# One decode step of attention and a gated feed-forward layer: batch rows packed side by side, K turned in one piece, fewer VectorE and GpSimd instructions

## The chip, the cores and the metric

The kernel runs on one core of a Trainium2 chip. The metric is the device time of one execution in microseconds (us); lower is better. Engines: TensorE (PE in the profile, PEld for its weight loads), VectorE (DVE), ScalarE (ACT), GpSimd (POOL), SyncE (SP), which here only issues loads, and sixteen DMA engines that move data between HBM and the on-chip memory (SBUF). Matrix products land in eight banks of PSUM.

## The reference

Four sequences (B = 4) each decode one token of width D = 576. Attention has 32 query heads, 16 key/value heads of width 128, and looks at the last 4096 of 16384 cached positions:

```python
W = min(4096, max(256, Sk // 4))                 # 4096
q = (layernorm(x) @ wq).reshape(B, 1, 32, 128).transpose(0, 2, 1, 3)
k = jnp.repeat(k_cache[:, :, Sk - W:, :], 2, axis=1)
v = jnp.repeat(v_cache[:, :, Sk - W:, :], 2, axis=1)
p = softmax(einsum("bhqd,bhkd->bhqk", q, k) * 128 ** -0.5)
h = x + einsum("bhqk,bhkd->bhqd", p, v).reshape(B, 1, 4096) @ wo
n = layernorm(h)
gate = n @ W_gate                                # 576 x 4608
out = h + ((gate * (gate > 0)) * (n @ W_up)) @ W_down
```

All inputs are bf16. The window of K is 4 x 16 x 4096 x 128 elements, 67 MB, and V as much; the weights are another 25 MB. Each byte is used once or by a few rows only.

## The kernel before

**Loads.** All large loads are issued by SP in one fixed order (`place`, `add_kv`, lines 219 to 290): wq, then K tiles 0 to 4, then V and K tiles in turn, the last four V tiles, wo, W_gate, W_up and W_down. One K or V tile is 4.19 MB: four heads of one sequence over the whole window (16 tiles each). K and V go round a ring of four slots in `arena`. Before SP issues a load it waits for the last reader of the place: the score products of a K tile (`QK`) or the value products of a V tile (`PV`). The weights at the end use slots that the last tiles release.

**Order of work.** Each engine runs its instructions in program order; the lists are written by `Prog`, with semaphore waits derived from named dependencies. The main loop goes over the 16 K tiles g, with batch b = g // 4:

- `turn_k` (line 427): VectorE turns the K tile in place by 32x32 blocks, taken as 32-bit words. A tile takes two instructions of 4096 columns (`TRA`). In tiles 4, 8 and 12 other work lies between the two.
- `pe_qk` (434): TensorE makes the scores of the tile, 32 products, once the second turn is done. Four tiles fill banks 0 and 1 with a batch's scores (128 x 1024).
- `soft` (459 to 480), once per batch: VectorE takes the row maximum (`MAX`), the maximum per head by two small turns (`MT`, `GM`, `GM1`, `MB`), scales it (`NB`); ScalarE takes exp in two halves of 512 with row sums (`EXP`); VectorE turns the two halves (`PTR`).
- `remap` (483 to 501): TensorE moves the probabilities to the layout that the value products need (`RM`), into banks 6 and 0; ScalarE copies the first half (`EV` 0, line 500), VectorE the second (`EV` 1, line 497), each in four copies, one per mask column of `m4`, into `pT`.
- `pe_pv` (504): 32 value products per V tile into banks 2 to 5. V runs four tiles behind K.
- `select_o` (524 to 536): the wanted rows of these banks, times the softmax weights `fm`, summed into `o_sel`, by ScalarE (line 529) and VectorE (532, 535, 536). It is put off until after the next K turn (`late`, `flush`).
- `weights` (540 to 551), once per batch: adds the two row sums (`WL`), spreads them over a mask (`FQ`), a product with `toq` on TensorE (`F4M`), reciprocal (`F4`), and `fm` (`FM`).

**Around it.** GpSimd makes masks and constants at the start (lines 293 to 336), among them `toq` by 16 selects (line 329); VectorE finishes some of them. After the loop come the output projection with wo, the second layer norm, gate and up products (line 675), the gated product `HH` (684), its transposes (690), the down projection (713), two final copies (716, 717) and two output stores of four rows each (720). In the feed-forward part the four batch rows stand in columns 0, 8, 16 and 24 of `hnT`, `sel4` and `xsel`, so the four output rows lie eight partitions apart.

Of the kernel before, what the change touches and what calls it, by code (L numbers as in the profile page):

```python
# [11 lines left out]
B = 4  # L12
# [110 lines left out]
def bass_sequential_preLN__sliding_block_cached__glu_gated_reglu__decode_kernel(  # L123
# [12 lines left out]
    with ExitStack() as es:  # L136
# [47 lines left out]
        gmh = sb("gmh", [128, 8], FP32)  # L184
        fq = sb("fq", [128, 4], FP32)
        f4 = sb("f4", [128, 4], FP32)
# [7 lines left out]
        xsel = sb("xsel", [B, 32], BF16)  # L194
# [97 lines left out]

        pool("c_idb0", lambda e: e.memset(ident_b[:, :], 0.0))
# [33 lines left out]
        pool("c_toq0", lambda e: e.memset(toq[:, :, :, :], 0.0))  # L327
        for q in range(16):
            pool(f"c_toq{q + 1}", lambda e, q=q: e.affine_select(out=toq[:, :, :, :], in_=toq[:, :, :, :],  # L329
                                                               pattern=[[0, 16], [-32, 4], [-1, 2]], compare_op=ALU.not_equal,  # L330
                                                               fill=1.0, base=-2 * q, channel_multiplier=1), [f"c_toq{q}"])
        pool("c_xs0", lambda e: e.memset(xsel[:, :], 0.0))
        pool("c_xs1", lambda e: e.affine_select(out=xsel[:, :], in_=xsel[:, :], pattern=[[-1, 32]], compare_op=ALU.not_equal,
                                                fill=1.0, base=0, channel_multiplier=8), ["c_xs0"])
        pool("c_oT", lambda e: e.memset(oT[:, :, :], 0.0))
        pool("c_hnT", lambda e: e.memset(hnT[:, :, :], 0.0))
        dve("c_eps", lambda e: e.memset(eps_c[:, :], EPS))
# [60 lines left out]
        def dve_x():  # L398
            dve(None, lambda e: e.tensor_copy(out=xnT[:, 0:4, 0:4], in_=tpv[:, 0:16].rearrange("p (c b) -> p c b", b=B)),
                ["TP1", "c_xnT"])  # L400
            for a in range(2):
                dve("xnT", lambda e, a=a: e.tensor_scalar(out=xnT[:, 4 + a, 0:4], in0=tpv[:, 16:20], scalar1=par[:, a:a + 1],
                                                          scalar2=None, op0=ALU.mult), ["c_par"])
            dve("xT", lambda e: e.tensor_copy(out=xT[:, :, :], in_=tpv[:, 32:52].rearrange("p (c b) -> p c b", b=B)))
# [22 lines left out]
        def turn_k(g, w):  # L427
            k = arena[:, land[("K", g)] + w * QWW:][:, 0:QWW].bitcast(FP32)
            dst = k.rearrange("p (n h l a) -> p n l h a", h=2, l=2, a=2)
            src = k.rearrange("p (n l h a) -> p n l h a", h=2, l=2, a=2)  # L430
            dve(("TRA", g, w), lambda e: e.transpose(out=dst, in_=src), [("L", "K", g)] if w == 0 else [])  # L431


        def pe_qk(g):
            b, qd = divmod(g, 4)
            for cb in range(4):
                for w in range(2):
                    for a in range(4):
                        deps = []
                        if cb == w == a == 0:  # L440
                            deps = [("TRA", g, 1)]
                            if g == 0:
                                deps.append("QW")
                            if qd == 0 and b:
                                deps += [("EXP", b - 1, 1), ("MAX", b - 1), ("EV", b - 1, 1)]
# [13 lines left out]
        def row_max(b):  # L459
            dve(("MAX", b), lambda e: e.tensor_reduce(out=hx[:, 0:1], in_=psb[:, 0:2, :].rearrange("p a b -> p (a b)"),  # L460
                                                      axis=AX.X, op=ALU.max, negate=True), [("QK", 4 * b + 3), "c_hx", ("NB", b - 1) if b else None])

        def head_max(b):
# [4 lines left out]
            dve(("GM1", b), lambda e: e.tensor_copy(out=hy[:, :].rearrange("p (d i q) -> p d i q", i=4, q=2),  # L468
                                                    in_=bass.AP(tensor=gmh, offset=0, ap=[[8, 128], [2, 4], [0, 4], [1, 2]])), [("GM", b)])
            dve(("MB", b), lambda e: e.transpose(out=hx[:, :], in_=hy[:, :]), [("GM1", b)])  # L470
            dve(("NB", b), lambda e: e.tensor_scalar(out=stat[:, b, 1:2], in0=hx[:, 0:1], scalar1=SCALE, scalar2=None, op0=ALU.mult),  # L471
                [("MB", b)])

        def exps(b):
            for w in range(2):
                act(("EXP", b, w), lambda e, w=w: e.activation(  # L476
                    out=p_sb[:, 512 * w:512 * w + 512], in_=bank[w], func=ACT.Exp, bias=stat[:, b, 1:2], scale=SCALE,
                    accum_out=stat[:, b, 5 + w:6 + w]), [("NB", b), ("PTR", b - 1, 1) if b else "QT"] if w == 0 else [])
            for w in range(2):
                dve(("PTR", b, w), lambda e, w=w: e.transpose(out=p2[:, 512 * w:512 * w + 512], in_=p_sb[:, 512 * w:512 * w + 512]),  # L480
                    [("EXP", b, w), ("RM", b - 1, 1) if b else None])

        def remap(b):
            for n in range(4):
                for i in range(4):
# [4 lines left out]
                        ([("PTR", b, 1), "c_tov", ("EV", b - 1, 0) if b else None] if n == 0 else [("EXP", b, 0)]) if n % 2 == i == 0 else [])  # L490
            for h in range(2):
                for a in range(4):
                    out_ = bass.AP(tensor=pp, offset=16 * h + 2 * a, ap=[[PPW, 128], [8, 2], [32, 128], [1, 2]])
                    src = bank[0 if h else 6].rearrange("p (n c q) -> p n c q", n=2, q=2)
                    deps = [("RM", b, h), ("PV", 4 * b - 1) if b else "QMM"] if a == 0 else []
                    if h:
                        dve(("EV", b, 1), lambda e, out_=out_, src=src, a=a: e.tensor_scalar(  # L497
                            out=out_, in0=src, scalar1=m4[:, a:a + 1], scalar2=None, op0=ALU.mult), deps)
                    else:
                        act(("EV", b, 0), lambda e, out_=out_, src=src, a=a: e.activation(  # L500
                            out=out_, in_=src, func=ACT.Copy, scale=m4[:, a:a + 1]), deps + (["c_m4"] if a == 0 else []))
# [38 lines left out]
        def weights(b):  # L540
            dve(("WL", b), lambda e: e.tensor_tensor(out=stat[:, b, 13:14], in0=stat[:, b, 5:6], in1=stat[:, b, 6:7], op=ALU.add),
                [("EXP", b, 0), ("EXP", b, 1)])
            dve(("FQ", b), lambda e: e.tensor_scalar(out=fq[:, :], in0=qm[:, :], scalar1=stat[:, b, 13:14], scalar2=None,  # L543
                                                     op0=ALU.mult), [("WL", b), "c_qm"])
            pe(("F4M", b), lambda e: e.matmul(m_ps[:, 0:4], lhsT=toq[:, :, :, :].rearrange("p j t h -> p (j t h)"), rhs=fq[:, :],  # L545
                                              start=True, stop=True), [("FQ", b), "c_toq16", "QT", "qkeep0", "qkeep1"])
# [24 lines left out]
        dve("c_sel", lambda e: e.tensor_reduce(out=sel4[:, 0:32:8], in_=c_s4[:, :, :], axis=AX.X, op=ALU.max),  # L571
            ["c_s41", "c_sel0"])
        for q in range(4):
            dve("c_selc", lambda e, q=q: e.tensor_copy(out=selc[:, q, :, q], in_=e8[:, :]), ["c_e8", "c_selc0"])
# [19 lines left out]
        for g in range(NTILE):  # L594
            turn_k(g, 0)
            if g == 4:
                soft(0)
            if g and g % 4 == 0:
                remap(g // 4 - 1)
            turn_k(g, 1)  # L600
# [12 lines left out]
        act("warm_sqrt2", lambda e: e.activation(out=warm[:, 0:1], in_=eps_c[:, :], func=ACT.Sqrt), [("EXP", B - 1, 1)])  # L613
# [139 lines left out]
```

## Time and profile before

| what | value |
|---|---|
| four runs | 380.13, 381.44, 380.27, 379.94 us; median 380.2 |
| profiled execution | 380.13 us, of which the span of the profile is 378.3 us |
| bytes read | 159.6 MB, 422 GB/s over the span |
| VectorE busy | 231.2 us, of which 140.7 us in the 32 K turns (4.43 us each) |
| TensorE busy | 210.9 us at a mean granted clock of 0.80 |
| ScalarE, GpSimd busy | 54.2 us, 21.9 us |
| first load issued, last weight products, final copies | 0.74, 373.96 to 375.3, 375.35 us |

In the profile's lines an instruction is named by engine, line and operation, with output and inputs and their shapes. The span begins with the first instruction and ends with the last; the time of the execution also holds what lies around it. In groups of instructions the numbers behind the bar are busy time, mean duration, and how long the engine stood idle before them, with what ended that idle time. DMA rows give the time from issue to landing, which holds the time in the queue behind earlier loads.

### The profile page before, as it was taken

Reading aid. Unit: us, or ns where it says so; the run is one execution under the profiler, and the core shown is the slowest. Engines: PE = TensorE matmul, PEld = TensorE weight load, DVE = VectorE, ACT = ScalarE, POOL = GpSimd, SP = SyncE. Lnnn points to the kernel's source line nnn. Section 1 sums busy time; section 2 is a strip of 40 time slices with the busy share of each in tenths; the row PEclk is TensorE's granted clock in tenths of the full one; section 3 lists DMA queues with packets and bytes.
Section 4 is the critical chain, followed back from the end, with each engine's and each line's share of the span. In section 5 each row is a group of like instructions: output and inputs, shape, how many; then the busy total and the mean of one; then the engine's idle time right before and its main releaser. Section 6 shows DMA issues by size and latency. Waiting matters only on the chain.

```text
span 378.3 us, 2653 instructions
## 1 busy us (share of the span) xinstructions
PE 210.9 (56%) x1456; PEld 39.2 (10%) x703; DVE 231.2 (61%) x206; ACT 54.2 (14%) x89; POOL 21.9 (6%) x44
## 2 busy tenths in 40 slices
PE   0404443239919191739292835574746597777665
PEld 0000000001101010101010100010101010004223
DVE  3278989779392959593838877766568524441220
ACT  3291000301010113010101130101010501120110
POOL 8860000000000000000000000000000000000000
PEclk9955666659979687778877885968797989996678
DMA  8999999999999999999999999999999999999994
GB/s 333 443 441 426 416 435 440 440 423 419 438 437 437 423 417 440 443 426 419 433 439 433 430 419 440 438 433 423 426 440 431 433 423 430 424 433 417 428 425 195
DMA packets 6660, 159.76 MB, mean 422 GB/s; under 512 B 748, under 2 KB 888, under 8 KB 1528
## 3 DMA queue, kind: packets, MB, share of 16 engines
q1 hardware_dynamic: 6632, 159.59, 98.4%
q8 instruction: 8, 0.13, 0.1%
q14 instruction: 4, 0.03, 0.0%
q10 hardware_dynamic: 16, 0.01, 0.0%
HBM read 159.58 MB, written 0.00 MB: 422 GB/s over the span
## 4 chain that ended last, share of the span: by engine, by line
DMA 61%; PE 18%; DVE 15%; issue 4%; SPq 1%
DMA sb_arena<-in_A_k_cache_dram 52%; DVE sb_arena L431 13%; PE psb L34 11%; DMA sb_arena<-in_B_W_down_dram 9%; PE psb L455 4%; PE psb L519 2%; DVE sb_o_tmp L532 1%; DVE sb_pp L497 1%; PE psb L545 0%; PE psb L713 0%; SPq L245 0%; PE psb L486 0%; SPq L287 0%; DVE sb_fq L543 0%; DVE sb_out_sb L716 0%
## 5 line engine op out<-in xcount | busy, mean ns | idle before, releaser
L431 DVE STREAM_TRANSPOSE sb_arena<-sb_arena 128x4096 f32<-128x4096 f32 x32 | 140.7, 4428 | 63.8 <-DMA sb_arena<-in_A_k_cache_dram 63.8
L34 PE MATMUL psb<-sb_arena,sb_pp 128*128 128x512 bf16 x382 | 104.9, 382 | 2.5 <-issue 2.4
L455 PE MATMUL psb<-sb_arena 128*32 128x512 bf16 x256 | 43.7, 640 | 107.5 <-DVE sb_arena L431 107.5
L519 PE MATMUL psb<-sb_arena,sb_pp 128*128 128x512 bf16 x115 | 44.0, 383 | 9.3 <-DVE sb_o_tmp L532 9.3
L34 PE MATMUL psb<-sb_arena 128*32 128x512 bf16 x256 | 44.7, 645 | 0.0
L529 ACT COPY sb_o_tmp<-psb 32x512 f32<-32x512 f32 x32 | 18.5, 578 | 180.5 <-PE psb L34 180.3
L532 DVE TENSOR_TENSOR sb_o_tmp<-psb,sb_fm 32x512 f32<-32x512 f32 x32 | 21.7, 678 | 16.9 <-PE psb L34 16.4
L455 PEld LDWEIGHTS psb<-sb_arena 128*32 128x32 bf16 x256 | 9.4, 118 | 150.7 <-DVE sb_arena L431 120.4
L519 PEld LDWEIGHTS psb<-sb_arena,sb_pp 128*128 128x128 bf16 x128 | 12.6, 99 | 113.2 <-issue 113.2
L536 DVE TENSOR_REDUCE sb_o_sel<-sb_o_tmp 128x128 f32<-128x512 f32 x16 | 17.7, 1103 | 0.5
L476 ACT ACTIVATE sb_pp<-psb,sb_stat 128x512 bf16<-128x512 f32 x8 | 5.4, 683 | 81.7 <-DVE sb_stat L471 81.7
L497 DVE TENSOR_SCALAR sb_pp<-psb,sb_m 128x512 bf16<-128x512 f32 x16 | 10.8, 739 | 4.7 <-PE psb L486 4.7
L329 POOL TENSOR_SCALAR_AFFINE_SELECT sb_toq<-sb_toq 128x128 f32<-128x128 f32 x16 | 12.7, 791 | 2.3
L500 ACT ACTIVATE sb_pp<-psb,sb_m 128x512 bf16<-128x512 f32 x16 | 9.7, 692 | 13.0 <-PE psb L486 13.0
L535 DVE TENSOR_TENSOR sb_o_tmp<-sb_o_tmp,sb_fm 64x512 f32<-64x512 f32 x16 | 11.0, 690 | 0.5
L422 ACT COPY sb_arena<-sb_q_keep 32x256 bf16<-32x256 bf16 x8 | 9.7, 1447 | 0.1
L545 PE MATMUL psb<-sb_fq,sb_toq 128*128 128x4 f32 x8 | 1.8, 300 | 12.6 <-DVE sb_fq L543 12.6
L486 PE MATMUL psb<-sb_pp,sb_to_v 128*32 128x256 bf16 x64 | 4.4, 402 | 6.0 <-DVE sb_pp L480 6.0
L713 PE MATMUL psb<-sb_arena,sb_pp 128*32 128x288 bf16 x72 | 7.0, 360 | 1.2 <-DMA sb_arena<-in_B_W_down_dram 1.2
L480 DVE STREAM_TRANSPOSE sb_pp<-sb_pp 128x512 bf16<-128x512 bf16 x8 | 5.5, 712 | 3.4 <-ACT sb_pp L476 3.4
L408 DVE CAST sb_pp<-psb 128x512 bf16<-128x512 f32 x1 | 2.4, 2428 | 7.6 <-PE psb L387 7.6
L684 DVE TENSOR_TENSOR sb_pp<-psb,sb_pp 128x384 bf16<-128x384 f32 x3 | 1.5, 550 | 8.9 <-PE psb L675 8.9
(126 smaller groups left out, 94.3 us busy)
## 6 DMA issues: line engine op xcount, KB each, us to landing
sb_arena<-in_A_k_cache_dram SPq DMA_DIRECT2D x16, 4096.0 KB, 26.1
sb_arena<-in_A_v_cache_dram SPq DMA_DIRECT2D x16, 4096.0 KB, 28.0
sb_arena<-in_A_wo_dram SPq DMA_DIRECT2D x1, 4608.0 KB, 26.1
sb_arena<-in_B_W_gate_dram SPq DMA_DIRECT2D x1, 4608.0 KB, 29.3
sb_arena<-in_A_wq_dram SPq DMA_DIRECT2D x1, 4096.0 KB, 12.2
sb_arena<-in_B_W_down_dram SPq DMA_DIRECT2D x3, 1296.0 KB, 33.4
sb_arena<-in_B_W_up_dram SPq DMA_DIRECT2D x1, 3456.0 KB, 30.3
sb_arena<-in_B_W_up_dram SPq DMA_DIRECT2D x1, 1152.0 KB, 32.7
```

The costliest lines, as they stand in the source:

```text
L34: return e.add_instruction(mybir.InstMatmult(name=e.bass.get_next_instruction_name(), engine=mybir.EngineType.PE, ins=[e.lower_ap(rhs), e. ...
L329: pool(f"c_toq{q + 1}", lambda e, q=q: e.affine_select(out=toq[:, :, :, :], in_=toq[:, :, :, :], pattern=[[0, 16], [-32, 4], [-1, 2]], com ...
L422: act("QW", lambda e, i=i, q=q: e.copy(out=bass.AP(tensor=arena, offset=32 * i * AW + 2 * i + q, ap=[[AW, 32], [512, 16], [136, 4], [32, 4]]),
L431: dve(("TRA", g, w), lambda e: e.transpose(out=dst, in_=src), [("L", "K", g)] if w == 0 else [])
L455: fn = lambda e, out_=out_, lhsT=lhsT, rhs=rhs, start=start, stop=stop: e.matmul(out_, lhsT=lhsT, rhs=rhs, start=start, stop=stop, skip_gr ...
L497: dve(("EV", b, 1), lambda e, out_=out_, src=src, a=a: e.tensor_scalar(out=out_, in0=src, scalar1=m4[:, a:a + 1], scalar2=None, op0=ALU.mu ...
L500: act(("EV", b, 0), lambda e, out_=out_, src=src, a=a: e.activation(out=out_, in_=src, func=ACT.Copy, scale=m4[:, a:a + 1]), deps + (["c_m ...
L519: fn = lambda e, lhsT=lhsT, rhs=rhs, k=k, j=j: e.matmul(bank[2 + j], lhsT=lhsT, rhs=rhs, start=(k == 0), stop=(k == 7), skip_group_check=True)
L529: act(("OSC", g), lambda e, j=j: e.copy(out=o_tmp[32 * j:32 * j + 32, 0:512], in_=bank[2 + j][32 * j:32 * j + 32, :]), [("PV", g), ("OSEL" ...
L532: dve(("OSD", g), lambda e, j=j: e.tensor_tensor(out=ot(32 * j, 32), in0=bank[2 + j][32 * j:32 * j + 32, :].rearrange("p (t d) -> p t d", ...
L535: dve(("OS", g), lambda e: e.tensor_tensor(out=ot(64, 64), in0=ot(64, 64), in1=fmb(64, 64), op=ALU.mult), [("OSC", g)])
L536: dve(("OSEL", g), lambda e: e.tensor_reduce(out=o_sel[:, qd, b, :], in_=o_tmp[:, 0:512].rearrange("p (t d) -> p d t", d=DH), axis=AX.X, o ...
```

## The change

Five groups of edits. First, K: a tile that has nothing between its two turns is turned by one instruction of 8192 columns; tiles 4, 8 and 12 keep two. Second, softmax: one exp of 1024 columns with one row sum per batch, one turn of the probabilities, the scale folded into `GM1`, the bias read from `hx`. The second half of the probabilities is copied by two products with a broadcast mask in place of four scaled copies, and `FQ` moves from VectorE to ScalarE, without `WL`. Third, constants: `toq` is made by two selects and one product with `par` on VectorE in place of 16 selects; `eps_c` is set by GpSimd in place of VectorE; `xsel` goes, the identity serves; `selc` is filled by one copy in place of four. Fourth, pairs of small instructions (`xnT`, `n3`) become one product with a broadcast. Fifth, the batch rows: columns 0 to 3 in `hnT` and `sel4`, so the output rows lie in neighbouring partitions.

```diff
+        pool("c_eps", lambda e: e.memset(eps_c[:, :], EPS))
         pool("c_idb0", lambda e: e.memset(ident_b[:, :], 0.0))
...
-        pool("c_toq0", lambda e: e.memset(toq[:, :, :, :], 0.0))
-        for q in range(16):
-            pool(f"c_toq{q + 1}", lambda e, q=q: e.affine_select(out=toq[:, :, :, :], in_=toq[:, :, :, :],
-                                                               pattern=[[0, 16], [-32, 4], [-1, 2]], compare_op=ALU.not_equal,
-                                                               fill=1.0, base=-2 * q, channel_multiplier=1), [f"c_toq{q}"])
-        pool("c_xs0", lambda e: e.memset(xsel[:, :], 0.0))
...
+        pool("c_toq0", lambda e: e.memset(toq[:, :, :, :], 1.0))
+        for sg in range(2):
+            pool(f"c_toq{sg + 1}", lambda e, sg=sg: e.affine_select(
+                out=toq[:, :, :, :], in_=toq[:, :, :, :],
+                pattern=[[0, 16], [32 * (1 - 2 * sg), 4], [0, 2]], compare_op=ALU.is_ge, fill=0.0, base=31 * (1 - sg), channel_multiplier=2 * sg - 1),
+                [f"c_toq{sg}"])
...
-        dve("c_eps", lambda e: e.memset(eps_c[:, :], EPS))
...
-        def turn_k(g, w):
-            k = arena[:, land[("K", g)] + w * QWW:][:, 0:QWW].bitcast(FP32)
+        def turn_k(g, lo, n):
+            k = arena[:, land[("K", g)] + lo * QWW:][:, 0:n * QWW].bitcast(FP32)
...
-            dve(("GM1", b), lambda e: e.tensor_copy(out=hy[:, :].rearrange("p (d i q) -> p d i q", i=4, q=2),
-                                                    in_=bass.AP(tensor=gmh, offset=0, ap=[[8, 128], [2, 4], [0, 4], [1, 2]])), [("GM", b)])
-            dve(("MB", b), lambda e: e.transpose(out=hx[:, :], in_=hy[:, :]), [("GM1", b)])
-            dve(("NB", b), lambda e: e.tensor_scalar(out=stat[:, b, 1:2], in0=hx[:, 0:1], scalar1=SCALE, scalar2=None, op0=ALU.mult),
-                [("MB", b)])
+            dve(("GM1", b), lambda e: e.tensor_scalar(out=hy[:, :].rearrange("p (d i q) -> p d i q", i=4, q=2),
+                                                    in0=bass.AP(tensor=gmh, offset=0, ap=[[8, 128], [2, 4], [0, 4], [1, 2]]),
+                                                      scalar1=SCALE, scalar2=None, op0=ALU.mult), [("GM", b)])
+            dve(("NB", b), lambda e: e.transpose(out=hx[:, :], in_=hy[:, :]), [("GM1", b)])
...
-            for w in range(2):
-                act(("EXP", b, w), lambda e, w=w: e.activation(
-                    out=p_sb[:, 512 * w:512 * w + 512], in_=bank[w], func=ACT.Exp, bias=stat[:, b, 1:2], scale=SCALE,
-                    accum_out=stat[:, b, 5 + w:6 + w]), [("NB", b), ("PTR", b - 1, 1) if b else "QT"] if w == 0 else [])
-            for w in range(2):
-                dve(("PTR", b, w), lambda e, w=w: e.transpose(out=p2[:, 512 * w:512 * w + 512], in_=p_sb[:, 512 * w:512 * w + 512]),
-                    [("EXP", b, w), ("RM", b - 1, 1) if b else None])
+            act(("EXP", b), lambda e: e.activation(out=p_sb, in_=psb[:, 0:2, :].rearrange("p a b -> p (a b)"), func=ACT.Exp,
+                                                   bias=hx[:, 0:1], scale=SCALE, accum_out=stat[:, b, 5:6]),
+                [("NB", b), ("PTR", b - 1) if b else "QT"])
+            dve(("PTR", b), lambda e: e.transpose(out=p2, in_=p_sb), [("EXP", b), ("RM", b - 1, 1) if b else None])
...
-                    if h:
-                        dve(("EV", b, 1), lambda e, out_=out_, src=src, a=a: e.tensor_scalar(
-                            out=out_, in0=src, scalar1=m4[:, a:a + 1], scalar2=None, op0=ALU.mult), deps)
...
+            for n in range(2):
+                dve(("EV", b, 1), lambda e, n=n: e.tensor_tensor(
+                    out=bass.AP(tensor=pp, offset=16 + 8 * n, ap=[[PPW, 128], [32, 128], [2, 4], [1, 2]]),
+                    in0=bass.AP(tensor=psb, offset=256 * n, ap=[[4096, 128], [2, 128], [0, 4], [1, 2]]),
+                    in1=bass.AP(tensor=m4, offset=0, ap=[[4, 128], [0, 128], [1, 4], [0, 2]]), op=ALU.mult),
+                    deps + [("RM", b, 1)] if n == 0 else [])
...
-            dve(("WL", b), lambda e: e.tensor_tensor(out=stat[:, b, 13:14], in0=stat[:, b, 5:6], in1=stat[:, b, 6:7], op=ALU.add),
-                [("EXP", b, 0), ("EXP", b, 1)])
-            dve(("FQ", b), lambda e: e.tensor_scalar(out=fq[:, :], in0=qm[:, :], scalar1=stat[:, b, 13:14], scalar2=None,
-                                                     op0=ALU.mult), [("WL", b), "c_qm"])
+            act(("FQ", b), lambda e: e.activation(out=fq[:, :], in_=qm[:, :], func=ACT.Copy, scale=stat[:, b, 5:6]), [("EXP", b), "c_qm"])
...
-        for q in range(4):
-            dve("c_selc", lambda e, q=q: e.tensor_copy(out=selc[:, q, :, q], in_=e8[:, :]), ["c_e8", "c_selc0"])
+        dve("c_selc", lambda e: e.tensor_copy(out=bass.AP(tensor=selc, offset=0, ap=[[128, 128], [33, 4], [4, 8]]),
+                                              in_=bass.AP(tensor=e8, offset=0, ap=[[8, 128], [0, 4], [1, 8]])), ["c_e8", "c_selc0"])
+        dve("c_toq", lambda e: e.tensor_tensor(out=toq[:, :, :, :], in0=toq[:, :, :, :],
+                                               in1=bass.AP(tensor=par, offset=0, ap=[[2, 128], [0, 16], [0, 4], [1, 2]]), op=ALU.mult),
+            ["c_toq2", "c_par"])
...
         for g in range(NTILE):
-            turn_k(g, 0)
-            if g == 4:
-                soft(0)
             if g and g % 4 == 0:
+                turn_k(g, 0, 1)
+                if g == 4:
+                    soft(0)
                 remap(g // 4 - 1)
-            turn_k(g, 1)
+                turn_k(g, 1, 1)
+            else:
+                turn_k(g, 0, 2)
             flush()
...
-        dve("n2", lambda e: e.tensor_copy(out=hnT[:, 0:4, 0:32:8], in_=tmp5[:, 0:4, :]), ["n2a", "c_hnT"])
-        for a in range(2):
-            dve("n3", lambda e, a=a: e.tensor_scalar(out=hnT[:, 4 + a, 0:32:8], in0=tmp5[:, 4, :], scalar1=par[:, a:a + 1], scalar2=None,
-                                                     op0=ALU.mult), ["n2a", "c_hnT"])
+        dve("n2", lambda e: e.tensor_copy(out=hnT[:, 0:4, 0:4], in_=tmp5[:, 0:4, :]), ["n2a", "c_hnT"])
+        dve("n3", lambda e: e.tensor_tensor(out=hnT[:, 4:6, 0:4], in0=bass.AP(tensor=tmp5, offset=16, ap=[[20, 128], [0, 2], [1, 4]]),
+                                            in1=bass.AP(tensor=par, offset=0, ap=[[2, 128], [1, 2], [0, 4]]), op=ALU.mult), ["n2a", "c_hnT"])
...
-            pe(None, lambda e, n=n: e.matmul(bank[n][32 * n:32 * n + 32, 0:288], lhsT=xsel[:, :], rhs=x_bf[:, 288 * n:288 * (n + 1)],
+            pe(None, lambda e, n=n: e.matmul(bank[n][32 * n:32 * n + 32, 0:288], lhsT=ident_b[0:B, 0:32], rhs=x_bf[:, 288 * n:288 * (n + 1)],
...
-                out=orow[:, 288 * n:288 * n + 288], in_=bass.AP(tensor=out_sb, offset=32 * n * 288, ap=[[8 * 288, 4], [1, 288]])),
+                out=orow[:, 288 * n:288 * n + 288], in_=out_sb[32 * n:32 * n + 4, :]),
```

## The prediction

> **What bounds the kernel now.** I read the summary first: which engine is near its limit over the whole span.
>
> ```profile
> span 378.3 us, 2653 instructions
> ...
> PE 210.9 (56%) x1456; PEld 39.2 (10%) x703; DVE 231.2 (61%) x206; ACT 54.2 (14%) x89; POOL 21.9 (6%) x44
> ...
> DMA  8999999999999999999999999999999999999994
> ...
> q1 hardware_dynamic: 6632, 159.59, 98.4%
> ...
> DMA 61%; PE 18%; DVE 15%; issue 4%; SPq 1%
> ```
>
> The reader is to see that no compute engine passes 61%, while the one DMA queue fills its sixteen engines for 98.4% of the span; its slices stay at nine from the second to the 39th. 159.59 MB move whatever the engines do. The chain of waits gives DMA only 61%, because it follows each load back to the compute that released its buffer. Whether that release comes late is the question, so I read stretches next (columns: stretch; busy us of PE, PEld, DVE, ACT, POOL; granted clock; DMA share; GB/s):
>
> ```profile
> 0.00:80.00 80.00, 21.70 (x202) 4.34 (x122) 56.41 (x47) 19.76 (x24) 21.93 (x44) 0.71 0.98 419
> 80.00:160.00 80.00, 51.03 (x315) 7.24 (x134) 56.00 (x41) 8.51 (x16) 0.00 (x0) 0.80 1.01 432
> 160.00:240.00 80.00, 46.95 (x282) 6.53 (x117) 55.46 (x41) 8.51 (x16) 0.00 (x0) 0.81 1.01 432
> 240.00:320.00 80.00, 50.75 (x278) 7.18 (x109) 48.59 (x46) 9.65 (x18) 0.00 (x0) 0.85 1.00 432
> ```
>
> Three stretches with different VectorE work have the same 432 GB/s. A K or V load of 4.19 MB therefore needs 4.19/0.432 = 9.7 us of the queue. How early are loads issued? From the page's issues and from the K/V issue line's time to landing:
>
> ```profile
> sb_arena<-in_A_wq_dram SPq DMA_DIRECT2D x1, 4096.0 KB, 12.2
> ```
>
> ```profile
> DMA to landing us min/median/max: 17.5/26.1/40.8
> ```
>
> The wq load has the same size and met an empty queue: 12.2 us. No K or V load landed in less than 17.5 us, so each found at least 17.5 - 12.2 = 5.3 us of other transfers ahead of it; the median found 13.9 us. The queue never ran dry. A compute stage that gets faster makes loads wait longer in the queue, and one that gets slower costs nothing until it eats 5.3 us.
>
> That leaves the end, where compute follows the last loads. The timeline there (start, duration, line, what ended the idle time):
>
> ```profile
> 354.32 0.51 PE L675 MATMUL psb<-sb_arena,sb_hnT 128*32 128x384 bf16 x4 [2.19 <-DVE sb_hnT L656]
> ...
> 359.82 0.35 PE L675 MATMUL psb<-sb_arena,sb_hnT 128*32 128x384 bf16 x4 [0.84 <-DMA sb_arena<-in_B_W_up_dram]
> ...
> 362.61 0.35 PE L675 MATMUL psb<-sb_arena,sb_hnT 128*32 128x384 bf16 x4 [1.14 <-DMA sb_arena<-in_B_W_up_dram]
> ...
> 371.90 1.28 PE L713 MATMUL psb<-sb_arena,sb_pp 128*32 128x288 bf16 x18 [0.41 <-DMA sb_arena<-in_B_W_down_dram]
> ...
> 373.96 1.36 PE L713 MATMUL psb<-sb_arena,sb_pp 128*32 128x288 bf16 x18 [0.78 <-DMA sb_arena<-in_B_W_down_dram]
> ```
>
> TensorE stands still for a weight load four times after 359 us. A compute chain that comes d later at 354 us moves the end only beyond 0.84 + 1.14 + 0.41 + 0.78 = 3.2 us, and one that comes earlier waits longer.
>
> **The change part by part.** The sum is made against the profiled execution: 378.3 us of span and 1.83 us around it, 380.13 us, 0.07 below the median of the four runs (380.2). No load changes in size, order or queue; SP's 46 load issues keep their order.
>
> *K turned in one piece* (13 of 16 tiles; tiles 4, 8 and 12 stay in two, with the softmax work in between). A turn of 4096 took 4.428 us and one of 32 columns 0.212 us, so (4.428 - 0.212)/4064 = 1.037 ns per column and 0.18 us fixed. Back to back a pair took 8.77 us; one of 8192 comes to 0.18 + 8.50 = 8.68. That is 0.09 us a tile, 1.2 us of VectorE in all, hidden by the 5.3 us of queue. Nothing stood between the two pieces in these tiles, so no instruction is held up longer. Bounds: 0 and 0.18 us a tile.
>
> *Softmax, per batch.* NB as an instruction of its own goes (0.154 us, about 0.2 with its wait; the scaling rides on GM1; the exp reads its bias from hx, so the next row maximum waits for it, which is done over 60 us earlier: 72 against 135 us). Two exps of 0.683 us with accumulator reads of 0.196 become one of 1024: ScalarE's slope from 288 columns at 0.399 to 512 at 0.578 is 0.80 ns, so 0.683 + 0.41 = 1.09 us. Two turns of 0.712 become one: 0.712 + 512 x 1.037 ns = 1.24 us. Before, the second exp ran beside the first turn and the pair took 2.2 us from exp to last turn (70.95 to 73.14); now nothing overlaps: 1.09 + 0.14 + 1.24 = 2.5 us. Net with NB: +0.1 us per batch, the one place where the change lengthens a chain.
>
> *The copy of P on VectorE* (L497): four tensor-scalar copies of 0.742 us, 2.73 us together, become two tensor-tensor products of 1024 from PSUM with a broadcast mask. No row has that form. Nearest: the product from PSUM of 32x512 at 0.681 us; 512 more columns at 1.04 ns give 1.21, and the scattered bf16 output adds 0.06 (0.742 against 0.681): 1.27 us each, 2.5 for both, 0.2 us less. Bounds: the same cost per column as now, 1.48 us each (+0.2 in all), and twice that, 2.97 us each, +3.2 us in all. I take 1.27.
>
> [...]
>
> Together a batch's softmax changes by -0.1 us; at the worst bound by +3.3.
>
> *Weights.* WL (0.124 us) goes; FQ moves from VectorE (0.230) to ScalarE, where rows of this size take 0.205 us. It stands there before L529's copies, behind exp and copies already done. TensorE waited for FQ behind the K turn for 12.6 us in three places; that goes, but the QK products behind it wait for the same turn (92.99 us, right after FQ at 92.39). Worth 0.3 to 0.6 us on a batch's QK release, hidden again.
>
> *GpSimd's toq.* Sixteen selects of 0.79 us (9.53 to 24.34) become two, plus a 128x128 product on VectorE: between 128x16 at 0.175 and 64x512 at 0.690 us, about 0.3. It is queued before the first K turn, which waits 2.33 us for its load at 23.92; the four selc copies merged there give back 0.87 minus about 0.2. Its reader comes at 92.67. Cost nothing; without that cover +0.3 minus 0.65. Moving eps to GpSimd's head delays its other constants by 0.10 us (a 128x1 memset) and with them, at most, ScalarE's table load wait and the load of x behind it; TensorE needs all this at 12.97, where it had waited 4.2 us for wq.
>
> *The tail.* Two n3 instructions (0.36 us) become one, about 0.18; the identity in place of xsel and rows side by side give the same matmuls. It is 0.2 us earlier at 354, swallowed by the W_up waits. The final copies keep 32x288. The output load takes 4 neighbouring partitions instead of every eighth: same rows and bytes. Bounds: SP waited 1.4 us for it, so -1.4; the load of x into four neighbouring rows took 4.7 us (0.90 to 5.56) against 2.5 here, so +2.2, but it shared the engines with the wq load. I take 0.
>
> *Instruction fetches* share the DMA engines: 4 packets, 0.03 MB, on queue q14. One engine moves 422/16 = 26.4 GB/s, so 8 KB is 0.3 us of one engine. Fewer instructions may drop one: 0 to -0.3, all four at the very best -1.2. I take 0.
>
> Sum: stream 0, tail 0, output 0: 380.13, forecast 380.1 us. VectorE falls from 231 to about 228 us and GpSimd from 22 to about 11, both unseen.
>
> **Rivals.**
>
> *Faster: compute traffic slows the DMA stream.* The first 80 us run at 419 GB/s, not 432; were that GpSimd's and VectorE's doing, removing their work would return up to 80 x (1 - 419/432) = 2.4 us: 377.7. Against it: the slices of five microseconds.
>
> ```profile
> 20.00:25.00 5.00, 0.00 (x0) 0.00 (x0) 2.66 (x9) 4.91 (x5) 4.28 (x8) 0.50 0.97 419
> 25.00:30.00 5.00, 0.00 (x0) 0.00 (x0) 5.00 (x2) 4.97 (x5) 0.85 (x2) 0.50 0.98 421
> 30.00:35.00 5.00, 2.26 (x20) 0.38 (x12) 3.60 (x2) 0.04 (x1) 0.00 (x0) 0.50 0.97 419
> ```
>
> With GpSimd busy for 4.3 of 5 us it is 419, with GpSimd idle also 419. What lowers the first stretch is the start, before the first bytes: the first five microseconds moved 250 GB/s. Together with the output and the fetches at their best ends: chance 0.12.
>
> *Slower: the new PSUM product is slow.* Place: the last batch's copy of P at 298.77 us, from which TensorE and VectorE run to 354 us without any wait for a load. Price: one for one beyond 3.2 us. It decides when the two products take over 2.73 + 3.2 = 5.9 us, 2.95 each, over twice my 1.27 and just about the doubled bound. At four times (5.1 each) the end comes 10.2 - 5.9 = 4.3 us later: 384.4. Earlier batches would join at 2.73 + 5.3 = 8.0 us. For it: eight-element inner runs with a broadcast, of which no row tells. Against it: the tensor-scalar row with the same scattered output pays only 0.06 us. With the output's bad end: chance 0.08.
>
> *The change does not do what it says on the stages* (merged pieces no shorter than their parts): the time is again 380.1, a part of the forecast.
>
> **How the numbers follow.** About 0.3%, 1.1 us, is what a measurement of this kernel can tell from no change; unchanged runs lay between 379.94 and 381.44. Forecast 0.80, faster rival 0.12, slower 0.08; these are also the chances by sign. The range reaches from 379.0 (380.1 less most of the fetches' bound) to 381.3 (the spread of unchanged runs) and holds the forecast; of the rivals it leaves out what lies beyond 0.3%.
>
> **What would show it.** Right: q1 again near 98%, stretches at 432 GB/s, shortest landing still above 17 us, the four weight-load waits of TensorE after 355 us still there and longer by some tenths, K turns of 8.6 to 8.8 us, products of about 1.3 us. Wrong: a stretch above 440 GB/s over 80 us, or a VectorE product near 3 us and no wait for W_up left; or an end after the last weight load that is not 4.3 us (374 to 378.3).

## The result and the profile after

The changed kernel takes 379.5 us (median of 33 runs, 379.28 to 380.6) against 380.17 us (53 runs): ratio 0.9984, 95% interval 0.9978 to 0.9991, or 0.6 us faster. That is inside the 0.3% that the prediction called no change and clear of zero. The profiled execution took 379.6 us, its span 377.5 us, 0.8 us less than before. The time shows less of this than the span, because what lies around the span grew: 2.08 us on average (2.02 to 2.13) over the runs of the changed kernel, 1.80 (1.75 to 1.87) over those of the kernel before.

The page of the changed kernel (summary and queues):

```profile
span 377.5 us, 2572 instructions
...
PE 209.1 (55%) x1456; PEld 37.7 (10%) x703; DVE 225.5 (60%) x164; ACT 54.3 (14%) x85; POOL 10.6 (3%) x29
...
DMA  8999999999999999999999999999999999999995
...
q1 hardware_dynamic: 6632, 159.59, 98.6%
...
q14 instruction: 2, 0.02, 0.0%
```

VectorE lost 5.7 us of work, GpSimd 11.3, two instruction fetches are gone, and the load queue is as full as before. Stretches (same columns as before) and time to landing of the K and V loads:

```profile
0.00:80.00 80.00, 22.17 (x202) 4.71 (x122) 54.44 (x35) 19.71 (x23) 10.60 (x29) 0.78 0.98 419
80.00:160.00 80.00, 50.62 (x313) 7.25 (x134) 55.08 (x32) 8.57 (x15) 0.00 (x0) 0.79 1.00 431
```

```profile
DMA to landing us min/median/max: 17.7/26.4/40.6
```

The first 80 us run at 419 GB/s with half of GpSimd's work gone: GpSimd was not what slowed them, and VectorE's 2.0 us less there did not show either. So the middle of the kernel gave nothing. The end of the changed kernel in its timeline:

```profile
355.58 0.51 PE L669 MATMUL psb<-sb_arena,sb_hnT 128*32 128x384 bf16 x4 [1.98 <-DVE sb_hnT L650]
...
362.55 0.35 PE L669 MATMUL psb<-sb_arena,sb_hnT 128*32 128x384 bf16 x4 [0.72 <-DMA sb_arena<-in_B_W_up_dram]
...
373.90 1.37 PE L707 MATMUL psb<-sb_arena,sb_pp 128*32 128x288 bf16 x18 [0.77 <-DMA sb_arena<-in_B_W_down_dram]
...
375.30 0.45 DVE L710 CAST sb_out_sb<-psb 32x288 bf16<-32x288 f32 x1 [9.69 <-PE psb L707]
...
375.76 0.28 ACTq L714 DMA_DIRECT2D out_dram<-sb_out_sb  x1
375.77 0.34 SPq L714 DMA_DIRECT2D out_dram<-sb_out_sb  x1
```

And the same two stores in the kernel before:

```profile
375.81 0.69 ACTq L720 DMA_DIRECT2D out_dram<-sb_out_sb  x1
375.83 0.75 SPq L720 DMA_DIRECT2D out_dram<-sb_out_sb  x1
```

The last products start at 373.90 against 373.96 us, the final copy at 375.30 against 375.35. Only then do the kernels part. The two stores, one on ScalarE's queue and one on SyncE's, take four rows each from four neighbouring partitions and are issued in 0.28 and 0.34 us, where four rows eight partitions apart took 0.69 and 0.75. From the start of SP's store issue to the end of the span it is 1.73 us instead of 2.47. The difference of 0.74 us is the 0.8 us of the span but for 0.06: 0.41 us of it lie in the issue, and SP's wait for the stores to land, the last of all, is 1.0 us where it was 1.4 (the kernel before first, then the changed one):

```profile
SPq L136 <- DMA out_dram<-sb_out_sb: 1.4, 1, 1.4
```

```profile
SPq L136 <- DMA out_dram<-sb_out_sb: 1.0, 1, 1.0
```

So somewhat less than half of the gain comes after the issue. Both kernels send eight packets a store. Before, the packets of the two stores went out near 377.2 and near 377.55 us, almost 0.4 us apart; in the changed kernel all went out between 376.5 and 376.75 us. Bytes, rows and packets are the same in both kernels. What the longer issue consists of, and why the packets of the second store follow so late with the rows eight apart, the traces do not show.

### The profile page after: what moved, and what is told of

The parts are those of the page before. It is cut to its first block, busy times and chain, and to the rows that moved or that the text cites. A ratio compares the mean times of both kernels' runs of the same rounds, so it can differ in the third digit from the quotient of the medians.

```text
span 377.5 us, 2572 instructions
## 1 busy us (share of the span) xinstructions
PE 209.1 (55%) x1456; PEld 37.7 (10%) x703; DVE 225.5 (60%) x164; ACT 54.3 (14%) x85; POOL 10.6 (3%) x29
## 4 chain that ended last, share of the span: by engine, by line
DMA 56%; PE 21%; DVE 20%; issue 1%; SPq 0%; ACT 0%
DMA sb_arena<-in_A_k_cache_dram 48%; DVE sb_arena L427 16%; PE psb L34 13%; DMA sb_arena<-in_B_W_down_dram 9%; PE psb L451 4%; PE psb L512 3%; DVE sb_o_tmp L525 1%; DVE sb_pp L490 1%; PE psb L478 1%; PE psb L707 0%; DVE sb_pp L473 0%; DVE sb_hx L456 0%; ACT sb_pp L470 0%; SPq L286 0%; DVE sb_out_sb L710 0%
## 5 line engine op out<-in xcount | busy, mean ns | idle before, releaser
L427 DVE STREAM_TRANSPOSE sb_arena<-sb_arena 128x8192 f32<-128x8192 f32 (+1 forms) x19 | 139.9, 7362 | 67.6 <-DMA sb_arena<-in_A_k_cache_dram 67.6
L34 PE MATMUL psb<-sb_arena,sb_pp 128*128 128x512 bf16 x382 | 107.0, 389 | 2.9 <-issue 2.8
L512 PE MATMUL psb<-sb_arena,sb_pp 128*128 128x512 bf16 x115 | 44.8, 390 | 8.9 <-DVE sb_o_tmp L525 8.9
L529 DVE TENSOR_REDUCE sb_o_sel<-sb_o_tmp 128x128 f32<-128x512 f32 x16 | 17.7, 1107 | 0.5
L470 ACT ACTIVATE sb_pp<-psb,sb_hx 128x1024 bf16<-128x1024 f32 x4 | 4.5, 1114 | 80.4 <-DVE sb_hx L467 80.4
L490 DVE TENSOR_TENSOR sb_pp<-psb,sb_m 128x1024 bf16<-128x1024 f32 x8 | 9.3, 1208 | 4.6 <-PE psb L478 4.6
L473 DVE STREAM_TRANSPOSE sb_pp<-sb_pp 128x1024 bf16<-128x1024 bf16 x4 | 5.0, 1245 | 5.1 <-ACT sb_pp L470 5.1
L707 PE MATMUL psb<-sb_arena,sb_pp 128*32 128x288 bf16 x72 | 5.2, 288 | 4.0 <-DMA sb_arena<-in_B_W_down_dram 4.0
L456 DVE TENSOR_REDUCE sb_hx<-psb 128x1 f32<-128x1024 f32 x4 | 4.9, 1225 | 2.3 <-PE psb L34 2.3
L34 PE MATMUL psb<-sb_arena,sb_hnT 128*32 128x384 bf16 x80 | 6.2, 394 | 0.0
```

Of the source, the lines that this page charges most:

```text
L34: return e.add_instruction(mybir.InstMatmult(name=e.bass.get_next_instruction_name(), engine=mybir.EngineType.PE, ins=[e.lower_ap(rhs), e. ...
L427: dve(("TRA", g), lambda e: e.transpose(out=dst, in_=src), [("L", "K", g)] if lo == 0 else [])
L490: dve(("EV", b, 1), lambda e, n=n: e.tensor_tensor(out=bass.AP(tensor=pp, offset=16 + 8 * n, ap=[[PPW, 128], [32, 128], [2, 4], [1, 2]]), ...
L512: fn = lambda e, lhsT=lhsT, rhs=rhs, k=k, j=j: e.matmul(bank[2 + j], lhsT=lhsT, rhs=rhs, start=(k == 0), stop=(k == 7), skip_group_check=True)
L529: dve(("OSEL", g), lambda e: e.tensor_reduce(out=o_sel[:, qd, b, :], in_=o_tmp[:, 0:512].rearrange("p (t d) -> p d t", d=DH), axis=AX.X, o ...
```

## The experiments

**Rows alone, and everything but the rows.** Three runs separate the last group of edits from the other four. The first is the kernel before with the rows side by side:

```diff
...
-        dve("c_sel", lambda e: e.tensor_reduce(out=sel4[:, 0:32:8], in_=c_s4[:, :, :], axis=AX.X, op=ALU.max),
+        dve("c_sel", lambda e: e.tensor_reduce(out=sel4[:, 0:4], in_=c_s4[:, :, :], axis=AX.X, op=ALU.max),
...
-        dve("n2", lambda e: e.tensor_copy(out=hnT[:, 0:4, 0:32:8], in_=tmp5[:, 0:4, :]), ["n2a", "c_hnT"])
+        dve("n2", lambda e: e.tensor_copy(out=hnT[:, 0:4, 0:4], in_=tmp5[:, 0:4, :]), ["n2a", "c_hnT"])
...
-                out=orow[:, 288 * n:288 * n + 288], in_=bass.AP(tensor=out_sb, offset=32 * n * 288, ap=[[8 * 288, 4], [1, 288]])),
+                out=orow[:, 288 * n:288 * n + 288], in_=out_sb[32 * n:32 * n + 4, :]),
```

> The kernel before with only the batch rows side by side (columns 0 to 3 in hnT, sel4 and xsel; the output stores read four neighbouring partitions). Store theory: the whole gain of the change lies in the two output stores, whose issue fell from 0.75 and 0.69 us to 0.34 and 0.28 and whose packets went out 0.6 us earlier, while the weight stream ended at the same moment. Then this kernel is 0.6 us faster than before (ratio 0.9984, within 0.9975 to 0.9992), with store issues of about 0.3 us. Rival, shorter engine work or fewer instruction fetches (two 8 KB fetches in place of four): this kernel is the same as before, 380.2 us, ratio 1.000.

Measured: 379.32 us, ratio 0.9982 (0.9972 to 0.9993). Its stores in the timeline:

```profile
376.92 0.28 ACTq L720 DMA_DIRECT2D out_dram<-sb_out_sb  x1
376.94 0.34 SPq L720 DMA_DIRECT2D out_dram<-sb_out_sb  x1
```

The whole gain is there, with 32 K turn instructions, 16 selects and all four instruction fetches still in place. (These two issues stand a microsecond later than above, because the last 18 products took 2.34 us in this execution, at a granted clock of 0.50, and not 1.37; see the two groups of runs below.)

The opposite: the changed kernel with the rows in columns 0, 8, 16 and 24 again.

```diff
...
-                out=orow[:, 288 * n:288 * n + 288], in_=out_sb[32 * n:32 * n + 4, :]),
+                out=orow[:, 288 * n:288 * n + 288], in_=bass.AP(tensor=out_sb, offset=32 * n * 288, ap=[[8 * 288, 4], [1, 288]])),
```

> The changed kernel with everything but the rows: they stand in columns 0, 8, 16, 24 again. Store theory: the same as before, ratio 1.000 within 0.0008, store issues of about 0.7 us. Rival, shorter engine work or fewer fetches: 0.6 us faster, ratio 0.9984. In both the K turns stay at 8.7 us and VectorE at about 226 us.

Measured: 380.1 us, ratio 1.0005 (0.9994 to 1.0017). All other edits together are worth nothing that can be measured in the time, and the issue is long again:

```profile
375.65 0.69 ACTq L718 DMA_DIRECT2D out_dram<-sb_out_sb  x1
375.67 0.75 SPq L718 DMA_DIRECT2D out_dram<-sb_out_sb  x1
```

That nothing is made of two parts: in the lower of the two groups of runs described below, the span is 378.0 us on average where the kernel before has 378.3, and what lies around the span is 2.06 us where it has 1.81. The other edits shorten the span by about 0.3 us and lengthen what lies around it by as much; what causes either is open.

**Distance or step?** The same with a step of two partitions (columns 0, 2, 4 and 6 in hnT and sel4):

```diff
...
-                out=orow[:, 288 * n:288 * n + 288], in_=out_sb[32 * n:32 * n + 4, :]),
+                out=orow[:, 288 * n:288 * n + 288], in_=bass.AP(tensor=out_sb, offset=32 * n * 288, ap=[[2 * 288, 4], [1, 288]])),
```

> The changed kernel with the rows in every second column, so the stores read every second partition. If the price lies in any step other than one between the rows, the store issues take 0.7 us again and the time is that of before (ratio 1.000). If it lies in how far apart the rows are, it is near the changed kernel (ratio 0.9984 to 0.999), with issues of 0.3 to 0.45 us. The rival of shorter engine work also says 0.9984, but with no tie to the store issues.

Measured: 380.17 us, ratio 1.0003 (0.9992 to 1.0014), and in its timeline:

```profile
376.66 0.70 ACTq L718 DMA_DIRECT2D out_dram<-sb_out_sb  x1
376.68 0.75 SPq L718 DMA_DIRECT2D out_dram<-sb_out_sb  x1
```

A step of two costs as much as a step of eight. The price goes with a step other than one, not with the distance; steps other than 1, 2 and 8 were not tried.

**The store or the layout of the tail?** In the kernel before, the stores alone read neighbouring partitions, and so three of the four output rows are left out:

```diff
-                out=orow[:, 288 * n:288 * n + 288], in_=bass.AP(tensor=out_sb, offset=32 * n * 288, ap=[[8 * 288, 4], [1, 288]])),
+                out=orow[:, 288 * n:288 * n + 288], in_=out_sb[32 * n:32 * n + 4, :]),
```

> The kernel before with only the two stores changed: they read four neighbouring partitions although the batch rows still stand eight apart, so the last three rows of the output are left out of the computation. Store theory: the full gain, 0.6 us, ratio 0.9984, without any change to the feed-forward layout. If the gain came from the columns of hnT and sel4 (the products and copies of the tail) instead, ratio 1.000.

Measured: 379.41 us, ratio 0.9982 (0.9971 to 0.9993). The store alone is the gain; the columns of hnT and sel4 matter only because they decide which partitions the store reads. In the lower group of runs the span falls to 377.5 us on average, with 1.80 us around it, so the store by itself is worth nearly 0.8 us; the changed kernel keeps 0.6 to 0.7 of it.

**Does the stream set the time?** Half of two V loads is left out, all engine work stays:

```diff
+            n = TILE // 2 if kind == "V" and g in (4, 5) else TILE
...
-                  lambda e: e.dma_start(out=arena[:, off:off + TILE], in_=src), key=f"slot{s}")
+                  lambda e: e.dma_start(out=arena[:, off:off + n], in_=src[:, :, 0:n]), key=f"slot{s}")
```

> The changed kernel with half of the loads of two V tiles (the fifth and sixth) left out: 2 x 2.1 MB = 4.19 MB less, all engine work as before on whatever stands in the buffers; so part of V is left out of the computation. Stream theory: 4.19 MB at 0.432 MB/ns are 9.7 us; the time falls by 9.7 us if compute can keep up, by less where the tail's compute chain (no load wait from 298 to 355 us) becomes the end; at least 3 us. Engine theory (the time is set by VectorE and TensorE and the buffers they release): no change, 379.5 us.

Measured: 370.35 us, ratio 0.9744 (0.9718 to 0.9771), 9.2 us below the changed kernel for an expected 9.7; the spans differ by 377.5 - 368.1 = 9.4. The stream sets the time nearly alone: 4.19 MB less is worth fifteen times what the change brought.

**How much cover is there in the tail?** Extra products in the last batch's copy of P write the same values again (shown for six; the other run has two):

```diff
-            for n in range(2):
-                dve(("EV", b, 1), lambda e, n=n: e.tensor_tensor(
+            ev = []
+            for n in (0, 1) * (4 if b == B - 1 else 1):
+                o = dve(("EV", b, 1), lambda e, n=n: e.tensor_tensor(
...
```

> The changed kernel with two more products in the last batch's copy of P on VectorE (the same values written again), 2 x 1.2 = 2.4 us later at 299 us. The forecast's cover in the tail: 3.2 us of waits for W_up and W_down before, 0.72 + 1.38 + 1.82 + 0.77 = 4.7 us in the changed kernel's profile. Forecast theory: no change against the changed kernel, 379.5 us, ratio 0.998 to 0.999 against before. Rival, the tail's compute sets the end (it has no load wait from 298 to 355 us): 2.4 us later, 381.9 us, ratio 1.0045.

Measured: 379.16 us, ratio 0.9973 (0.9961 to 0.9984). 2.4 us more in this chain cost nothing: the profiled span is 377.4 us. The run is even 0.3 us below the changed kernel, which again lies around the span: 1.75 us on average there instead of 2.08.

> As the run with two more products, with six: 7.3 us later at 299 us. Forecast theory: cover of 3.2 to 4.7 us is used up, the end comes 2.6 to 4.1 us later than in the changed kernel: 382.1 to 383.6 us, ratio 1.005 to 1.009, with no wait for W_up left. Rival, compute sets the end: 386.8 us, ratio 1.017. Third possibility, the weights too come later because their buffers are freed later: also near 386.

Measured: 380.03 us, ratio 0.9993 (0.9982 to 1.0004): about 0.5 us more than the changed kernel by the medians and 0.9 by the spans of the profiled executions (378.4 against 377.5), not 2.6 to 4.1. The last products and the copy in its timeline:

```profile
371.54 4.59 PE L709 MATMUL psb<-sb_arena,sb_pp 128*32 128x288 bf16 x72
376.16 0.45 DVE L712 CAST sb_out_sb<-psb 32x288 bf16<-32x288 f32 x1 [5.10 <-PE psb L709]
```

All 72 down products now run in one piece without a wait, so the cover is indeed used up. The gate products had begun at 362.02 instead of 355.58 us, 6.4 later; the copy came 0.86 later, at 376.16 instead of 375.30. From there on 5.6 us of delay were swallowed, more than the 4.7 us that the listed waits add up to. The idle times of the waits do not hold all that a chain gives back: the 72 products in one piece took 4.59 us, where with three waits (1.38, 1.82, 0.77) they took 375.27 - 366.08 = 9.2, so 4.6 came back and not 3.97.

**How much cover has the queue?** Extra products in the first batch alone, four and eight (shown for four, the rest as above):

```diff
...
+            for n in (0, 1) * (3 if b == 0 else 1):
...
```

> The changed kernel with four more products in the first batch's copy of P only (at 74 us), 4 x 1.2 = 4.8 us. This holds up the fifth K tile's turn and with it the release of the buffers whose loads were issued at 85.7 and 92.9 us, the place with the shortest queue. Forecast theory: at least 5.3 us of other transfers lie ahead of each load, so the queue does not run dry: 379.5 us, ratio 0.998 to 0.999, with the shortest time to landing down from 17.7 to about 13 us. Rival, any delay at this place is paid: 384.3 us, ratio 1.011.

> As the run with four more products in the first batch, with eight: 9.7 us at 76 us. Forecast theory: 9.7 less 5.3 to 6.5 us of cover: the stream stops for 3.2 to 4.4 us and the end comes that much later, 382.7 to 383.9 us, ratio 1.007 to 1.010, with the shortest time to landing at 12.2 us, that of an empty queue. If the cover were larger (compute catches up elsewhere): no change. Rival, any delay is paid: 389.2 us, ratio 1.024.

Measured: 381.09 us for four, ratio 1.0020 (1.0004 to 1.0037); 384.13 us for eight, ratio 1.0092 (1.0076 to 1.0108). For four, no change had been expected: a miss. For eight, 382.7 to 383.9 us had been expected, with a shortest landing of 12.2 us. The slice behind the late loads (kernel with four first, then with eight; columns as in the stretches):

```profile
90.00:95.00 5.00, 5.00 (x24) 0.59 (x6) 4.43 (x1) 0.00 (x0) 0.00 (x0) 1.00 1.00 367
```

```profile
90.00:95.00 5.00, 4.58 (x36) 0.77 (x18) 5.00 (x2) 0.00 (x0) 0.00 (x0) 0.62 0.18 79
95.00:100.00 5.00, 5.00 (x25) 0.54 (x6) 3.80 (x1) 0.00 (x0) 0.00 (x0) 1.00 0.94 367
```

In the changed kernel the first of these slices moved 459 GB/s. With eight products the queue stands still. Time to landing of the K and V loads in that kernel:

```profile
DMA to landing us min/median/max: 13.9/26.2/40.4
```

The shortest is the load issued at 94.21 us into the empty queue; VectorE began to turn it at 108.13. So 13.9 us is what a K load takes from an empty queue in the middle of the kernel, not the 12.2 us of the first load. By that the cover is 17.7 - 13.9 = 3.8 us. For eight it fits: with eight products the load of 85.68 us was issued at 94.21, 8.5 late; less 3.8 it is 4.7 us, and 384.13 - 379.5 = 4.6 were measured. With four it was issued at 89.79, 4.1 late, where 3.8 would leave 0.3, and that load's turn did begin just 0.3 us later (103.71 against 103.41); measured were 1.6 by the medians, with single runs spread from 380.19 to 382.89, and 1.2 by the spans of the profiled executions (378.7 against 377.5), both with 1.37 us for the last 18 products. The trace shows where most of it lies: from 70 to 115 us the kernel with four moved 421 GB/s, the changed kernel 431 and the kernel with eight 385. Over 45 us that is 0.45 and 2.07 MB less, or 1.0 and 4.8 us of the stream at 432 GB/s. In the kernel with four the slice from 92 to 93 us moved only 98 GB/s, so its queue all but ran dry although the load was no later than 4.1 us. The 3.8 us are therefore an upper bound; about 3 us is what the kernel with four leaves. Why its single runs spread so far stays open.

**The two groups of runs.** Runs of both kernels fall into two groups a microsecond apart: 33 of the changed kernel have 21 between 379.28 and 379.6 and 12 between 380.27 and 380.6; before likewise near 380.05 and 381.1. In the profiled executions the last 18 products took 1.36 to 1.37 us in the lower group (before, after, rows apart by eight) and 2.34 to 2.35 in the upper one (rows alone, rows apart by two, store alone), at a granted clock of 1.00 and 0.50. The changed kernel was run again beside one that loads the last part of W_down in four pieces:

```diff
-            for r0, r1 in ((0, 9),) if j < 3 else ((0, 6), (6, 8), (8, 9)):
+            for r0, r1 in ((0, 9),) if j < 3 else ((0, 3), (3, 6), (6, 8), (8, 9)):
...
-                        if r == 0 or (j == 3 and r in (6, 8)):
+                        if r == 0 or (j == 3 and r in (3, 6, 8)):
```

> The changed kernel once more, beside the next one on the same chip: ratio 0.998, its runs in two groups one microsecond apart, near 379.45 and 380.45 us (before: 380.05 and 381.1). Clock theory: the groups differ by the last 18 products, which take 1.37 us at full granted clock and 2.34 us at half.

Measured: 379.46 us, ratio 0.9987 (0.9978 to 0.9997); 8 runs from 379.27 to 379.58, 3 from 380.47 to 380.57. The profiled one was of the upper group (380.5 us); its timeline, and the clock in the stretch from 374 us:

```profile
371.66 4.50 PE L707 MATMUL psb<-sb_arena,sb_pp 128*32 128x288 bf16 x36 [1.81 <-DMA sb_arena<-in_B_W_down_dram]
...
376.19 0.45 DVE L710 CAST sb_out_sb<-psb 32x288 bf16<-32x288 f32 x1 [10.94 <-PE psb L707]
```

```profile
374.00:376.00 2.00, 2.00 (x19) 1.07 (x14) 0.00 (x0) 0.00 (x0) 0.00 (x0) 0.50 0.03 10
```

> The changed kernel with the first six rows of the last W_down part loaded in two pieces of three, so that six of the last 18 products can run about a microsecond earlier, while the load behind them is still in flight. Clock theory: at half clock the end of the products moves from 2.34 us after the wait to about 1.55 (the load of the last piece ends the chain, then two products), so the upper group of runs comes down by 0.8 to 0.95 us and nearly joins the lower one, which stays at 379.45: all runs within 379.2 to 379.8, ratio 0.9975 to 0.998. If the two groups come from something else (the stream, what lies around the span), the upper group stays at 380.45. [...]

Measured: 379.52 us, ratio 0.9982 (0.9973 to 0.9991), and all 11 runs from 379.28 to 379.62. The upper group is gone, as the clock theory said; the lower one did not move. With the share of 12 in 33 that the changed kernel had, eleven independent runs without one of the upper group would come by chance in fewer than one case in a hundred. Against the changed kernel the median is the same and the mean of the runs falls from 379.7 to 379.5 us. Its profiled execution had a granted clock of 1.00 from 371 us to the last products:

```profile
373.90 0.55 PE L707 MATMUL psb<-sb_arena,sb_pp 128*32 128x288 bf16 x6 [0.48 <-DMA sb_arena<-in_B_W_down_dram]
374.61 0.66 PE L707 MATMUL psb<-sb_arena,sb_pp 128*32 128x288 bf16 x6 [0.16 <-DMA sb_arena<-in_B_W_down_dram]
```

Where 18 products stood behind the last long wait, 12 do, in two steps. Whether other runs had half the clock and a shorter way, as expected, or full clock throughout, is not shown by any profile.

## Why the prediction was right, and where not

*The stream.* Right. Left out bytes come back nearly one for one, engine work does not: the change without its rows stands at 1.0005. That this is so close to 1 is in part luck, since the prediction also took the 1.83 us around the span as fixed, and the other edits moved span and surroundings by about 0.3 us each, in opposite directions.

*The single costs.* Most held. In the groups of the changed kernel by form:

```profile
L427 DVE STREAM_TRANSPOSE sb_arena<-sb_arena 128x8192 f32<-128x8192 f32 x13 | 113.3, 8713 | 62.6 <-DMA sb_arena<-in_A_k_cache_dram 62.6
...
L490 DVE TENSOR_TENSOR sb_pp<-psb,sb_m 128x1024 bf16<-128x1024 f32 x8 | 9.3, 1208 | 4.6 <-PE psb L478 4.6
...
L473 DVE STREAM_TRANSPOSE sb_pp<-sb_pp 128x1024 bf16<-128x1024 bf16 x4 | 5.0, 1245 | 5.1 <-ACT sb_pp L470 5.1
...
L470 ACT ACTIVATE sb_pp<-psb,sb_hx 128x1024 bf16<-128x1024 f32 x4 | 4.5, 1114 | 80.4 <-DVE sb_hx L467 80.4
...
L534 ACT ACTIVATE sb_fq<-sb_qm,sb_stat 128x4 f32<-128x4 f32 x4 | 1.2, 300 | 0.1
```

The one-piece turn took 8.71 us (8.68 forecast), the turn of the probabilities 1.245 (1.24), the exp 1.11 (1.09), the product from PSUM 1.21 (1.27); FQ on ScalarE 0.30 instead of 0.205. VectorE fell to 225.5 us where 228 was forecast; the prediction's own terms add up to about 226, so the 228 was mis-added and not mis-measured. GpSimd fell to 10.6 (11). None of it shows in the time. The two products took 2.35 us together where the four copies had taken 2.73, so 0.4 us a batch was gained on VectorE and not 0.2.

*The output.* This is the term that failed: "I take 0" for the store, between bounds of -1.4 and +2.2. It measured -0.74 us from the start of SP's store issue to the end of the span. The prediction argued from rows and bytes, which are the same; what differs is the issue, 0.34 us with neighbouring partitions and 0.75 otherwise, and the wait behind it, 1.0 us and 1.4. Both stand behind the last copy, with nothing beside them, and are paid in full. The forecast of no change held because 0.74 us is 0.2% of the time, not because the term was right. Of the signs of being wrong that were named in advance, one appeared, "an end after the last weight load that is not 4.3 us": it was 377.5 - 373.9 = 3.6.

*The covers.* Both were mis-sized, in opposite directions. The queue's 5.3 us rested on the first load's 12.2 us as the time from an empty queue; in the middle of the kernel that is 13.9, which leaves 3.6 (17.5 - 13.9; 3.8 in the changed kernel) at most. The tail's 3.2 us was the sum of four waits; 5.6 us were swallowed from 355 us on. Part of that difference is the clock: from 366 to 371 us TensorE was granted 0.50 in the kernel before and 1.00 in the changed one, and its waits for W_down were 1.2 and 4.0 us. Neither error mattered, since the change itself lengthens no chain by more than tenths.

*The tail's waits.* "Longer by some tenths" did not hold for each. In the profiled execution the compute chain came 1.3 us later at 355 us and the first W_up wait all but vanished, while those for W_down grew. TensorE's granted clock from 300 to 310 us was 0.66, before 0.83. The same kernel profiled again began its gate products at 354.00 us, so one execution differs from the next by as much, and the change is not shown to be the cause. The end did not move, which shows the cover once more.

*The rivals.* The faster rival's mechanism (compute traffic slows the stream) fell with the unchanged 419 GB/s, as far as GpSimd's traffic goes; VectorE's hardly changed. The slower rival needed a product near 3 us; it took 1.21, and even the six added ones, 7.3 us, cost only 0.5.

## What to carry to other kernels

When a load queue is full from start to end, look for gains in fewer bytes and behind the last load; here 4.19 MB less took 9.2 us off, and 0.74 us less between the start of the last store's issue and the end took 0.8 us off the span. Give the rows of a final store neighbouring partitions (issued in 0.34 us on SyncE's queue, with a step of two or eight in 0.75), and let as few products as possible wait for the last piece of weights (12 in place of 18 brought the mean of the runs from 379.7 to 379.5 us). The cover of a queue is at most the shortest time to landing less that of a load that truly met an empty queue at that place; the first load at the start, 12.2 us where the load in the middle took 13.9, was too kind a measure. Compare spans beside times: a change can move what lies around the span, here by 0.3 us.

## What the runs showed of the hardware

A store of four rows from on-chip memory was issued in 0.27 to 0.28 us on ScalarE's queue and 0.34 to 0.35 on SyncE's with a partition step of one, in 0.69 to 0.70 and 0.75 with a step of two or eight. With a step of one (the changed kernel) the packets of the two stores, issued 0.01 us apart, went out together, within 0.25 us; with a step of eight (the kernel before) those of the second store, issued 0.02 us after the first, came almost 0.4 us later.

The two groups of runs a microsecond apart come from TensorE's clock in the last two microseconds: 0.50 or 1.00 was granted to the same products in the same order after a wait of 0.76 to 0.78 us in all six profiled executions named above. What decides between the two rates these runs do not show.
